# One kernel, one edit: the third block's weight quads in another order, with twelve weight sums read where they were made

## The chip, the cores and the metric

The kernel runs on one core of one Trainium2 chip. The time is the device time of one execution in microseconds; the measured figure is the median over several executions. A core has a matrix engine (TensorE, PE in the profile, with its weight loads as PEld), VectorE (DVE), ScalarE (ACT), GpSimd (POOL) and SyncE (SP). Each has its own instruction stream; they meet in semaphores. Weights and activations lie in on-chip memory (SBUF); TensorE writes into eight accumulation banks (PSUM, numbered 0 to 7), which another engine must read out before they are opened again. Transfers between DRAM and SBUF are issued by SP, ACT or POOL.

## What is computed

The input `x` is 2048 rows of 1024 values. Everything is in bfloat16 outside, and the output is bfloat16.

```python
xn = layernorm(x)                                   # over the 1024 values, no gain or offset
# branch A: a diagonal state space model with 1024 complex states
dt = exp(log_dt);  Lam = Lambda_re + 1j * Lambda_im
Lam_bar = exp(dt * Lam)
B_bar = ((Lam_bar - 1) / Lam)[:, None] * (B_re + 1j * B_im)
Bu = xn @ B_bar.T
h_t = Lam_bar * h_(t-1) + Bu_t                      # over the 2048 rows
y = 2 * real(hseq @ (C_re + 1j * C_im).T) + xn * Dskip
# branch B: a layer of width 3584
z = mish(xn @ w1 + b1) @ w2                         # mish(h) = h * tanh(softplus(h))
out = x + y + z
```

## The kernel before

**Five queues.** The program doesn't issue instructions as it goes. It records each operation in one of five lists (class `Queue`, L91), with the buffers that it reads and writes; from these it derives the semaphore waits, and at the end `emit` (L130) writes each list out as one engine's instruction stream. So the order of the calls in the source is the order on every engine, and an instruction that waits holds up everything that is behind it on its own engine.

**Blocks.** The rows are worked in four blocks of 512. For each block: layernorm; the product with `w1` and, between its parts, the product with the input matrix B; Mish; the scan over the rows; the products with `w2` and with C into the same banks; the output. The first block is plain. The second takes 12 of its 28 tiles of `w1` plainly and the other 16 as four quads (below). The third and the fourth block take all 28 as seven quads. The change is in the third block, whose product with `w1` and B, "the projection", runs in the profile from 306.6 to 373.5 us, and whose output products end at 446.8 us.

**Quads and units.** A quad is four tiles of `w1`, 512 columns. Columns and the inner dimension are halved, and the four quarter products are made with seven multiplications in place of eight (Strassen's scheme in Winograd's form). Each multiplication is a unit, numbered 1 to 7: eight matmuls of 128x256. Units 1, 2 and 4 use weights as they are; units 5, 6, 7 and 3 use sums and differences of weights, made by VectorE (`w_sums`, L1191, the instruction at L1199), always in the order 5, 7, 6, 3. Each is written over one of the raw quarters on chip and then stored to DRAM (array `wsd`) by POOL, except that the stores of group 2 are kept back and issued by SP. The stored units are loaded again for later blocks. The matching sums of the activations are in `TT`. The product with B is cut the same way into four parts of seven units.

**The letters.** The order within a projection is written by hand in strings, one for each block (`STEPS`, L196, for the third). A letter and a number is a step. `p q s w x y z` with 1 to 7 are units of the seven quads, `a b c d` with 1 to 7 those of the product with B. `k0` makes the next sum that is due (first the twelve of the `w1` groups 2, 0 and 1, four each, in this order; then sums for `w2`). `m1` loads raw rows of `w2` by POOL, `h` scales such a row on ScalarE (L1240), which POOL then stores (L1230). `g` is the Mish over a quad's results (L894), preceded by its table load. `r` is a step that prepares the scan on VectorE (L910), `E` the layernorm statistics of one quarter of the next block's rows (L564), `G` a scaling of activations, `t` sums of activations, `S` a scaling of rows, and `l0` the loads of the next block's `x`, four DMAs on POOL (L398). `O0` issues a store that was kept back, on SP: block outputs and the sums of group 2. `D` and `kp` belong to the part after the projection.

`project_fast` (L1368) reads such a string. For each unit `w_product` (L998) records the matmuls (L1024) and `w_evacuate` (L1030) at once what reads the bank out: a snapshot to SBUF on ScalarE (L1044) or on VectorE (L1047, always two instructions), or a join with an earlier snapshot on VectorE (L1061). For B these are `product` (L948 the matmuls), and `evacuate` with copies on VectorE (L963) and ScalarE (L965) and joins (L973).

**Banks.** Each quad has three banks. Unit 1 opens the first, and 6, 7 and 4 add to it; unit 2 opens the second, unit 5 the third, and 3 adds to that. Which three is in `W_BANKS` (L206), in the order of the quads:

```python
W_BANKS = ((0, 2, 1), (3, 2, 4), (7, 2, 6), (3, 5, 7), (1, 5, 6), (4, 5, 7), (3, 5, 6))
```

A unit that opens a bank waits until its last user's result has been read out; one that adds to it waits until the snapshot of the sum so far is out.

**The ring.** Weights come through a ring of seven slots of 512 KB, in the order of use, by SP (`ring_load` L426, `ring_fill` L856). One slot holds two units, each a load of 256 KB. When the last unit of a slot has been used, the slot's place goes to the next item of the list. One group of the second block reads its sums where VectorE made them (`ON_CHIP`); in the third block every unit is loaded through the ring, also those of groups 0, 1 and 2, whose sums are made early in this very projection and go to DRAM and back.

**Which quad is which group.** `REAL` (L207) is (3, 4, 5, 6, 0, 1, 2): in the third and fourth block `p` is group 3, and the groups 0, 1 and 2 are the last three quads, `x`, `y` and `z`.

**Behind the projection** the third block runs `tail` (L1495): matmuls for the fast part of `w2` (L1563) and for its plain part and C (L1502); results kept aside by VectorE in `KS` (L1580) or by ScalarE; scans on VectorE (L1453); and at the end the sums into the output (L1707).

Of the kernel before, what the change touches and what calls it, by code (L numbers as in the profile page):

```python
# [5 lines left out]
ALU = mybir.AluOpType  # L6
# [3 lines left out]
P = 128  # L10
# [153 lines left out]
def build_kernel(nc, A_x, A_Lambda_re, A_Lambda_im, A_B_re, A_B_im, A_C_re, A_C_im,  # L164
# [22 lines left out]
    W2_ORDER = (*range(9), 13, *range(9, 13))  # L187
    EARLY, LATE = ((0, 18), (26, 28)), ((18, 26),)
# [3 lines left out]
    WHOLE = ("a2 a1 V0 b2 b1 a5 b5 V1 P4 P5 a6 b6 v6 P6 P7 a3 b3 P0 a7 b7 P1 Q0 n0 p1 q1 a4 b4 "  # L192
# [6 lines left out]
    LAST = ("p1 p5 p2 q1 q5 p6 q2 s1 p7 s5 p3 q6 s2 M5 p4 q7 q3 k0 k0 s6 q4 g0 K0 a2 a1 k0 s7 k0 s3 O0 O0 O0 O0 m6 b2 b1 s4 G1 G0 g1 a5 G3 b5 G2 a6 b6 "  # L199
# [11 lines left out]
    OPENS = [(REAL[QUADS.index(o[0])], int(o[1])) for o in WHOLE.split() if o[0] in QUADS]  # L211
    OPENS = [u for u in OPENS if u not in ON_CHIP]
    O_ITEMS = [("w1", f // 2) for f in TILES[::2]] + [("ws", tuple(OPENS[i:i + 2])) for i in range(0, len(OPENS), 2)]
# [198 lines left out]
    items = []  # L412
    for blk in range(NB):
        items += W_ITEMS if blk in SPLIT else O_ITEMS if blk == FAST else [("w1", g) for g in range(NF // 2)]
# [8 lines left out]
        items += [("c", j) for j in range(NJ)] if blk >= FAST else []  # L423
    n_loaded = [0]
# [175 lines left out]
    def plain_root():  # L600
        aop(lambda e: e.activation(ln[:, 3, :], mv[:, :, 1], AF.Sqrt, bias=kon[:, 2:3]), reads=b_mv + [b_kon], writes=b_ln[3])
        vop(lambda e: e.reciprocal(ln[:, 3, :], ln[:, 3, :]), reads=b_ln[3], writes=b_ln[3])
        vop(lambda e: e.scalar_tensor_tensor(out=ln[:, 4, :], in0=mv[:, :, 0], scalar=-1.0, in1=ln[:, 3, :], op0=ALU.mult, op1=ALU.mult),
            reads=b_mv + b_ln[3], writes=b_ln[4])
# [245 lines left out]
    n_item = [0]  # L850

    def item_done():
        n_item[0] += 1
        ring_fill()
# [8 lines left out]

    def first_tile(blk, f):
        bank = f % 8
        raw = blk == 0 and f < NR
        if raw:
            first_rest(f)
        for k in range(0 if raw else NK):
            s, w = w1_tile(n_item[0], f % 4, k)  # L870
            PE.mm(lambda e, k=k, w=w: e.matmul(ps[:, bank, :], lhsT=w, rhs=xnT[:, k, :],  # L871
                                               start=k == 0, stop=k == NK - 1),
                  reads=[b_ring[s]] + b_xnT, writes=[b_ps[bank]], first=k == 0, last=k == NK - 1)
        if f % 4 == 3:
            item_done()
            item_done()
        at = place(blk, f)
        ts = slice(2 * P if raw else 0, 4 * P)
        aop(lambda e: e.activation(at[0][:, ts], ps[:, bank, ts], AF.Mish, bias=b1(f)),
            reads=[b_ps[bank], b_par], writes=[at[1]])  # L880
# [113 lines left out]
    def w_out(blk, i, ci):  # L994
        f0 = 4 * i + 2 * ci
        return f0, *(places(SPLIT[0], f0, 2) if blk in SPLIT else places(blk, 4 * REAL[i] + 2 * ci, 2))

    def w_product(blk, i, n):  # L998
# [3 lines left out]
        direct = blk == FAST and (REAL[i], n) in ON_CHIP  # L1002
        if direct:
            unit, b_unit = w_unit(w_raw(REAL[i], *((1, 1), (0, 0), (0, 1), (1, 0))[(5, 6, 3, 7).index(n)]))
        else:
            kind, units = items[n_item[0]]
# [20 lines left out]
        if not direct and half == len(units) - 1:  # L1027
            item_done()
# [219 lines left out]
    def d2_scale(g):  # L1248
        for n in range(4):
            d2_row(4 * g + n)  # L1250
# [789 lines left out]
```

## Time and profile before

| | |
|---|---|
| times of three executions | 588.1, 587.55, 587.74 us |
| median | 587.74 us |
| profiled execution, span | 586.3 us |
| TensorE busy | 581.0 us, 99% of the span |
| VectorE busy | 513.4 us, 88% |
| ScalarE busy | 401.8 us, 69% |
| GpSimd busy | 150.7 us, 26% |
| moved by DMA | 162.15 MB, mean 277 GB/s |

The profile is of one execution. Its span, 586.3 us, is from the first to the last instruction; no device time is given for that execution itself, and the three times are of others. Times in the rows count from the start of the span. A row of the timeline gives the start, the duration, the engine, the line of the code, the operation, what it writes and reads, the shape and how many instructions are drawn together (x8); in brackets stands how long the engine was idle before it, and for whom it waited. A row of a stretch of time gives the stretch, its length, and then for TensorE, its weight loads, VectorE, ScalarE and GpSimd the busy time and the number of instructions, and at its end the granted clock of TensorE, the share of time that the DMA engines were busy, and GB/s. A row of waits gives who waited for whom, the sum in us, the count and the mean. A row of DMAs gives the transfer, who issued it, the count, the size and the median time from issue to landing.

Consecutive matmuls overlap, and their ends are modelled; their starts are what the hardware recorded.

### The profile page before, as it was taken

To read this page: it belongs to the slowest core of one execution; us is meant where nothing else is said; L and a number is where in the kernel's file an instruction comes from. 1 tells how busy PE (TensorE), PEld (TensorE's weight loads), DVE (VectorE), ACT (ScalarE), POOL (GpSimd) and SP (SyncE) were. 2 spreads that over 40 slices of the span, in tenths; PEclk is the share of its full clock that TensorE was granted. 3 is DMA by queue.
4 is the path that set the end of the run, shared out by engine and by line. 5 is a ranking of instruction groups with operands and counts; after the bars stand their busy time and mean duration, and the time that the engine had idled before them with its cause. 6 is when DMAs were issued, how large, how long until landed. Compare 5 with 4: busy or idle time off the path is not lost.

```text
span 586.3 us, 9768 instructions
## 1 busy us (share of the span) xinstructions
PE 581.0 (99%) x3599; PEld 353.9 (60%) x3635; DVE 513.4 (88%) x789; ACT 401.8 (69%) x541; POOL 150.7 (26%) x213
## 2 busy tenths in 40 slices
PE   9999999999999999999999999999999999999998
PEld 8644444444447887444448888644446888844444
DVE  6998999998997878999877889779999669789995
ACT  4859994658578868999916687959223798992330
POOL 2899300123524420441351241001010113100000
PEclk9999999999999999999999999999999999999999
DMA  9999998999688978999999899798865966998832
GB/s 244 306 243 247 245 186 202 316 301 360 185 303 287 357 249 293 316 321 255 345 375 345 305 309 382 257 344 209 306 210 191 346 237 241 326 324 318 293 113 73
DMA packets 116345, 162.15 MB, mean 277 GB/s; under 512 B 55882, under 2 KB 66762, under 8 KB 116298
## 3 DMA queue, kind: packets, MB, share of 16 engines
q1 hardware_dynamic: 99776, 109.67, 62.0%
q0 software_dynamic: 13440, 44.57, 21.7%
q10 hardware_dynamic: 3082, 7.29, 3.3%
q8 instruction: 29, 0.48, 0.3%
q14 instruction: 18, 0.15, 0.1%
HBM read 115.36 MB, written 34.08 MB: 255 GB/s over the span
## 4 chain that ended last, share of the span: by engine, by line
PE 93%; DVE 2%; ACT 2%; DMA 1%; issue 1%; POOL 0%; ACTq 0%; POOLq 0%
PE ps L1502 34%; PE ps L1024 19%; PE ps L948 13%; PE ps L1563 10%; PE ps L871 10%; PE ps L1438 5%; DMA act<-in_A_B_im_dram 1%; PE ps L680 1%; PE ps L689 1%; PE ps L642 1%; ACT act L894 1%; PE ps L1525 1%; ACT act L901 1%; DVE CT L835 0%; DVE CT L833 0%
## 5 line engine op out<-in xcount | busy, mean ns | idle before, releaser
L1502 PE MATMUL ps<-ring,act 128*128 128x512 bf16 x532 | 117.3, 379 | 0.6
L1502 PEld LDWEIGHTS ps<-ring,act 128*128 128x128 bf16 x544 | 53.2, 98 | 63.8
L1044 ACT ACTIVATE snaps<-ps,par,cs 128x256 f32<-128x256 f32 x100 | 54.4, 562 | 44.4 <-PE ps L1024 40.0
L1502 PE MATMUL ps<-ring,hT 128*128 128x512 bf16 x355 | 78.3, 379 | 0.4
L1024 PE MATMUL ps<-TT,ring 128*128 128x256 f16 x552 | 68.3, 273 | 0.0
L910 DVE TENSOR_TENSOR mt<-hT,tab 128x2048 bf16<-128x2048 bf16 (+1 forms) x56 | 67.9, 1213 | 0.4
L1502 PEld LDWEIGHTS ps<-ring,hT 128*128 128x128 bf16 x362 | 35.4, 98 | 42.7
L1453 DVE TENSOR_TENSOR_SCAN hT<-cs,qi,hT 128x512 bf16<-128x512 f32 x48 | 60.7, 1275 | 0.0
L1024 PEld LDWEIGHTS ps<-TT,ring 128*128 128x128 f16 (+1 forms) x552 | 53.8, 98 | 7.2 <-issue 0.2
L871 PE MATMUL ps<-xnT,ring 128*128 128x512 bf16 x258 | 56.8, 379 | 0.3
L1024 PE MATMUL ps<-xnT,ring 128*128 128x256 bf16 x424 | 53.9, 273 | 0.0
L1061 DVE SCALAR_TENSOR_TENSOR act<-ps,cs,snaps 128x512 bf16<-128x512 f32 x54 | 39.8, 748 | 15.2 <-PE ps L1024 13.3
L1024 PEld LDWEIGHTS ps<-xnT,ring 128*128 128x128 bf16 (+1 forms) x424 | 41.4, 98 | 5.4
L871 PEld LDWEIGHTS ps<-xnT,ring 128*128 128x128 bf16 x264 | 25.8, 98 | 30.9
L1230 POOL DMA_DIRECT2D w2d<-act x21 | 15.0, 718 | 110.5 <-ACT act L1240 54.9
L1473 ACT ACTIVATE hT<-hT,wz 128x1024 bf16<-128x1024 bf16 x16 | 18.1, 1146 | 34.3 <-DVE hT L1468 34.3
L1563 PE MATMUL ps<-ring,act 128*128 128x512 bf16 (+1 forms) x176 | 39.5, 379 | 0.2
L1230 POOL DMA_DIRECT2D w2d<-hb x28 | 20.0, 717 | 74.4 <-ACT hb L1240 33.0
L894 ACT ACTIVATE act<-act 128x2048 bf16<-128x2048 bf16 (+3 forms) x13 | 33.0, 2557 | 3.8 <-DVE act L1047 3.8
L973 DVE TENSOR_TENSOR hT<-ps,snaps 128x512 f16<-128x512 f32 x36 | 23.8, 687 | 12.3 <-ACT snaps L965 11.1
L1563 PEld LDWEIGHTS ps<-ring,act 128*128 128x128 bf16 (+1 forms) x180 | 17.6, 98 | 20.6
L1173 POOL DMA_DIRECT2D wsd<-hb x35 | 19.1, 548 | 39.0 <-DVE hb L1199 28.8
(240 smaller groups left out, 1085.2 us busy)
## 6 DMA issues: line engine op xcount, KB each, us to landing
ring<-wsd SPq DMA_DIRECT2D x122, 256.0 KB, 4.6
ring<-in_B_w_dram SPq DMA_DIRECT2D x54, 512.0 KB, 5.9
ring<-ctd SPq DMA_DIRECT2D x24, 512.0 KB, 4.4
ring<-w2d SPq DMA_DIRECT2D x24, 512.0 KB, 4.6
wsd<-hb POOLq DMA_DIRECT2D x35, 256.0 KB, 5.1
ring<-w2d SPq DMA_DIRECT2D x29, 256.0 KB, 3.8
w2d<-hb POOLq DMA_DIRECT2D x28, 256.0 KB, 5.5
w2d<-act POOLq DMA_DIRECT2D x21, 256.0 KB, 6.2
```

Of the source, the lines that this page charges most:

```text
L871: PE.mm(lambda e, k=k, w=w: e.matmul(ps[:, bank, :], lhsT=w, rhs=xnT[:, k, :], start=k == 0, stop=k == NK - 1), reads=[b_ring[s]] + b_xnT, ...
L894: aop(lambda e: e.activation(t, t, AF.Mish), reads=b, writes=b)
L910: vop(lambda e: e.tensor_tensor(mt[:], u.unsqueeze(1).to_broadcast([P, 2, 2, TB]), tab[:, :, j, :].unsqueeze(2).to_broadcast([P, 2, 2, TB] ...
L948: PE.mm(lambda e, w=w, x=x, o=o, begin=begin, end=end: e.matmul(ps[:, bank, o:o + TH], lhsT=w, rhs=x, start=opens and begin, stop=end, ski ...
L1024: PE.mm(lambda e, w=w, x=x, o=o, begin=begin, end=end: e.matmul(ps[:, bank, o:o + TH], lhsT=w, rhs=x, start=opens and begin, stop=end, ski ...
L1044: aop(lambda e, o=o, p=p, j=j: e.activation(o, p, AF.Identity, scale=ig, bias=b1(f0 + j)), reads=[b_ps[b], b_par, b_ig], writes=b_dst)
L1061: vop(lambda e: e.scalar_tensor_tensor(out=dst, in0=bank(b), scalar=ig, in1=src, op0=ALU.mult, op1=ALU.add), reads=[b_ps[b], b_snap[k], b_ ...
L1230: PO.dma(lambda e: e.dma_start(w2d[at // 4][:, at % 4 * TB:(at % 4 + 2) * TB].rearrange("p (j t) -> p j t", j=2), t[:, :, d, :]), sem, rea ...
L1438: PE.mm(lambda e, j=j, ci=ci, k=k, bank=bank: e.matmul(ps[:, bank + ci, :], lhsT=BT[:, ci, j, k, :], rhs=xnT[:, k, :], start=k == 0, stop= ...
L1453: vop(lambda e: e.tensor_tensor_scan(out=hT[:, ci, j, :], data0=cj("r", j).to_broadcast([P, TB]), data1=hT[:, ci, j, :], initial=init, op0 ...
L1502: PE.mm(lambda e: e.matmul(ps[:, u, :], lhsT=lhsT, rhs=rhs, start=st_, stop=last, skip_group_check=blk in SPLIT), reads=reads, writes=[b_p ...
L1563: PE.mm(lambda e: e.matmul(ps[:, bank, :], lhsT=lhsT, rhs=rhs, start=st_, stop=end, skip_group_check=True), reads=b_t + [b_ring[s]], write ...
```

## The change

Four things change, all in the third block or in how its order is written.

1. `REAL` becomes (3, 2, 0, 1, 4, 5, 6). In the third and fourth block the quads `q`, `s` and `w` are now groups 2, 0 and 1, and `x`, `y` and `z` are 4, 5 and 6. The second block keeps its groups (`group`).
2. In the third block units 5, 6, 3 and 7 of groups 2, 0 and 1 are read from the buffers where VectorE made them, not through the ring (`ON_CHIP`). So 12 items of 256 KB are no longer in this block's list. The stores to DRAM stay, for the fourth block.
3. The fourth quad, `w`, stands before and among the first units of the product with B. Before, it came behind all four parts but the last units of `c` and `d`.
4. The order is written out further. What reads a bank out is a step of its own (`ep1` for `p1`), and no longer follows the unit at once; and what lies behind the projection, until the block's output, stands in the same strings. One loop, `perform`, runs all four blocks. A slot of the ring is given on when its last use has been recorded, counted for each item (`used`, `release`). Stores of sums that were kept back and stores of outputs that were kept back are two lists (`O` and `o`).

For the second half of the third block the new string moves, among others: the preparing step `r4` in between the two `KS` steps `kp0` and `kp1`, some scans ahead of others, and the statistics `E3` behind the first half of unit 7 of `w2` (`D70`). The number of matmuls is the same in every block, and the strings for the other three blocks give the order that they had.

The core of the diff:

```diff
-    W2_ORDER = (*range(9), 13, *range(9, 13))
-    EARLY, LATE = ((0, 18), (26, 28)), ((18, 26),)
+    W2_ORDER = tuple(range(14))
+    EARLY, LATE = ((0, 20),), ((20, 28),)
...
-    STEPS = ("p1 p5 p2 k0 k0 q1 k0 q5 p6 k0 q2 s1 k0 p7 s5 p3 k0 q6 s2 p4 k0 q7 q3 k0 s6 q4 m1 k0 g0 a2 a1 k0 s7 O0 s3 O0 b2 b1 k0 O0 s4 g1 k0 O0 a5 "
-             "b5 O0 a6 b6 O0 a3 h4 b3 S0 O0 a7 O0 h5 b7 k0 c2 d2 k0 h6 a4 b4 h7 l0 k0 c5 c1 k0 d5 d1 r0 c6 G0 c3 G1 d6 d3 c7 G2 w1 d7 r1 w5 w2 G3 c4 d4 k0 E0 E1 w6 x1 x5 x2 k0 w7 k0 w3 r2 "
-             "x6 w4 k0 y1 y5 y2 x7 x3 E2 E3 y6 x4 z1 z5 g2 z2 y7 y3 z6 G7 y4 g6 z3 z7 u0 t0 G8 u2 G9 z4 I2 G10 u1 t1 t2")
+    STEPS = ("p1 p5 ep1 ep5 p2 ep2 k0 k0 q1 eq1 p3 k0 q5 p6 q2 k0 ep6 eq2 s1 eq5 O0 k0 ep3 p7 es1 O0 ep7 s5 es5 k0 O0 q6 eq6 s2 es2 O0 p4 ep4 k0 q7 eq7 s6 "
+             "q3 eq3 k0 es6 q4 eq4 g0 k0 s7 s3 es7 o0 w1 ew1 es3 o0 s4 es4 k0 w2 m1 o0 o0 k0 w5 k0 ew2 b1 ew5 b2 eb2 eb1 w6 ew6 w3 b5 eb5 ew3 w7 ew7 ea2 "
+             "a2 g1 a1 ea1 b6 eb6 w4 ew4 a5 b3 h4 ea5 eb3 a6 h5 b7 ea6 eb7 S0 ec2 a3 a7 ea7 k0 ea3 k0 h6 c2 d2 a4 ea4 ed2 b4 h7 c5 eb4 ec5 c1 ec1 k0 d5 "
+             "ed5 d1 ed1 k0 r0 c6 ec6 G0 G1 c3 ec3 d6 ed6 d3 ed3 c7 G2 ec7 l0 x1 ex1 r1 d7 G3 ed7 x5 ex5 c4 x2 E1 ex2 ec4 k0 d4 E0 ed4 x6 y1 ex6 ey1 y5 "
+             "ey5 k0 y2 ey2 x7 ex7 x3 ex3 y6 r2 x4 ey6 ex4 k0 E2 z1 ez1 z5 ez5 z2 y7 y3 ez2 ey7 ey3 z6 z3 ez6 g2 k0 y4 ey4 G7 g6 ez3 z7 G9 ez7 D10 D11 G8 "
+             "z4 t0 ez4 G10 D70 E3 t1 t2 kp2 r3 D20 D71 kp0 g7 r4 G4 lr0 G12 D21 li0 X5 kp1 G5 r5 r6 r7 G11 ns0 X6 kp3 pl24 ns2 pl10 ns1 G6 tr0 ns3 tr1 "
+             "tr2 pl8 tr3 ph8 sc20 sc00 pl22 sc21 ph22 G13 pl12 pl26 sc50 sc01 sc10 to0 sc11 so0 al0 ta0 X3 to1 so1 sc30 al1 to2 sc41 sc31 so2 to3 sc60 "
+             "sc40 al2 so3 sc71 to4 X4 so4 sc51 to5 so5 al4 k0 sc70 al3 sc61 al5 to6 so6 jk0 to7 so7 sk0 al7 sk1 sk2 sk3 al6 Y0 sx0 sx1 sx2 sx3 k0 Y1 Y2 "
+             "Y3 Y4 Y5 k0 Q0 fin0 Q1 fin1 ax2 ax3 Q2 fin2 Q3 fin3")
...
-    REAL = (3, 4, 5, 6, 0, 1, 2)
-    UNITS = [(REAL[QUADS.index(o[0])], int(o[1])) for o in STEPS.split() if o[0] in QUADS]
-    W_ITEMS = [("ws", tuple(UNITS[i:i + 2])) for i in range(0, len(UNITS), 2)]
-    ON_CHIP = [(5, n) for n in (5, 6, 3, 7)]
...
+    REAL = (3, 2, 0, 1, 4, 5, 6)
+
+    def group(blk, i):
+        return REAL[i] if blk in SPLIT else i + 3
+
+    def fetched(blk, order, made):
+        us = [(group(blk, QUADS.index(o[0])), int(o[1])) for o in order.split() if o[0] in QUADS and len(o) == 2 and o[1].isdigit()]
+        us = [u for u in us if u not in made]
+        return [("ws", tuple(us[i:i + 2])) for i in range(0, len(us), 2)]
+
+    ON_CHIP = {FAST: [(5, n) for n in (5, 6, 3, 7)], SPLIT[0]: [(g, n) for g in (2, 0, 1) for n in (5, 6, 3, 7)], NB - 1: []}
...
-    def item_done():
-        n_item[0] += 1
-        ring_fill()
...
+    def used(i):
+        left[i] -= 1
+        if left[i] == 0:
+            gone.add(i)
+            return True
+        return False
+
+    def release():
+        while n_item[0] in gone:
+            n_item[0] += 1
+            ring_fill()
...
     def w_product(blk, i, n):
...
-        direct = blk == FAST and (REAL[i], n) in ON_CHIP
+        g = group(blk, i)
+        direct = (g, n) in ON_CHIP[blk]
         if direct:
-            unit, b_unit = w_unit(w_raw(REAL[i], *((1, 1), (0, 0), (0, 1), (1, 0))[(5, 6, 3, 7).index(n)]))
+            unit, b_unit = w_unit(w_raw(g, *((1, 1), (0, 0), (0, 1), (1, 0))[(5, 6, 3, 7).index(n)]))
...
-        if not direct and half == len(units) - 1:
-            item_done()
+        if not direct and used(at):
+            release()
```

More of the change, by code (lines that the diff above doesn't have):

```diff
@@ L411, in build_kernel @@
     NT = 7 * (NF // 2)
[L412 removed]
+    items, item_blk = [], []
     for blk in range(NB):
[L414 removed]
+        items += W_ITEMS[blk] if blk in SPLIT else O_ITEMS if blk == FAST else [("w1", g) for g in range(NF // 2)]
         if blk == NB - 1:
@@ L850, in build_kernel @@
     n_item = [0]
-    def item_done():
-        n_item[0] += 1
-        ring_fill()
+    at_item, left, gone = {}, {}, set()
+    for i_, (kind_, g_) in enumerate(items):
+        b_ = item_blk[i_]
+        if kind_ == "ws":
+            for u_ in g_:
+                at_item[b_, "ws", u_] = i_
+            left[i_] = len(g_)
+        elif kind_ == "tp":
+            for h_, u_ in enumerate(g_):
+                at_item[b_, "tp", u_] = i_, h_
+            left[i_] = 4 * len(g_)
+        else:
+            at_item[b_, kind_, g_] = i_
+            left[i_] = 2 * min(4, NT - 4 * g_) if kind_ == "ts" else 16
+    def used(i):
[8 more added lines that the diff above has]
+            ring_fill()
     def ring_fill():
@@ L862, in ring_fill @@
             ring_load()
[L864 to L874, printed above, removed]
-            item_done()
[L876 to L880, printed above, removed]
     def places(blk, f, n):
@@ new lines, in perform @@
+        for o in (FIRST, WHOLE, STEPS, LAST)[blk].split():
+            kind = o.rstrip("0123456789.")
+            arg = o[len(kind):]
+            if kind in ("D", "X"):
+                a = arg.split(".")
+                ks = range(int(a[1]), int(a[2])) if len(a) > 1 else range(ng)
+                n, i = (int(a[0][0]), (int(a[0][1]),)) if kind == "D" else (int(a[0]), (0, 1))
+                rows(n, i, ks)
+            elif len(kind) == 1 and kind in QUADS:
+                w_product(blk, QUADS.index(kind), int(arg))
+            elif len(kind) == 1 and kind in "abcd":
+                product(blk, "abcd".index(kind), int(arg))
+            elif len(kind) == 2 and kind[0] == "e" and kind[1] in QUADS:
+                w_evacuate(blk, QUADS.index(kind[1:]), int(arg), keep)
+            elif len(kind) == 2 and kind[0] == "e" and kind[1] in "abcd":
+                evacuate("abcd".index(kind[1:]), int(arg), keep, kind[1:] in "ab" and blk != FAST)
+            else:
+                run[kind](int(arg or 0))
@@ L2005, in build_kernel @@
+        assert near or not (steps or later), (len(steps), len(later))
+    for blk in range(NB):
+        perform(blk)
     SP.wait(out_events.values())
```

763 lines of the change are left out of this document (265 added, 498 removed), and 30 rows, old and new, of tables (FIRST, LAST, WHOLE).

## The prediction

> **What bounds the kernel now.** I read the page's busy times first, then the same by stretches, then who waited for whom on TensorE.
>
> ```profile
> span 586.3 us, 9768 instructions
> PE 581.0 (99%) x3599; PEld 353.9 (60%) x3635; DVE 513.4 (88%) x789; ACT 401.8 (69%) x541; POOL 150.7 (26%) x213
> 306.60:373.50 66.90, 66.89 (x610) 59.43 (x609) 57.16 (x97) 49.33 (x72) 15.93 (x25) 1.00 0.97 335
> PE ps L642 <- DVE filler L468: 1.0, 1, 1.0
> PE ps L680 <- ACT xr L527: 0.2, 1, 0.2
> ```
>
> The third row is the projection of the third block (us from 306.6 to 373.5): TensorE 66.89 of 66.90 us, clock 1.00, DMA share 0.97. The last two rows are all that TensorE is shown to wait for, both at the start. So the sum of the matmuls sets the time, and another engine counts only where it is too late for TensorE. Small waits hide in the modelled ends, so I take them from starts, in the timeline of TensorE:
>
> ```profile
> 306.68 1.04 PE L1024 MATMUL ps<-xnT,ring 128*128 128x256 bf16 x8
> 307.56 1.04 PE L1024 MATMUL ps<-TT,ring 128*128 128x256 f16 x8
> 308.43 1.91 PE L1024 MATMUL ps<-xnT,ring 128*128 128x256 bf16 x16
> 311.92 1.91 PE L1024 MATMUL ps<-xnT,ring 128*128 128x256 bf16 x16
> 313.79 1.91 PE L1024 MATMUL ps<-TT,ring 128*128 128x256 f16 x16
> 332.27 1.92 PE L948 MATMUL ps<-xnT,SS 128*128 128x256 bf16 x16
> 372.45 1.04 PE L1024 MATMUL ps<-TT,ring 128*128 128x256 f16 x8
> ```
>
> A unit (eight matmuls) takes 0.873 us: six of them lie between 306.68 and 311.92. Unit k of the third block should start at 306.68 + 0.8735 (k-1). The 76th, z7, starts at 372.45 instead of 372.19: all waits of this projection are worth 0.26 us. About half is before p7 (due 313.67, started 313.79), half before a3 (332.27).
>
> **The change, part by part.**
>
> *Work.* Each block keeps its seven-product units, tiles, w2 products and output products; only order and source change. TensorE's sum of matmuls is unchanged. The most that can be won in the third block is the 0.26 us.
>
> *Twelve loads less.* Units 5, 6, 3 and 7 of groups 2, 0 and 1 come from where VectorE left them; 12 loads of 256 KB (3.1 MB) go from SP's queue. TensorE waits for no load, so this is worth nothing in itself. The stores stay, because the last block fetches these units.
>
> *New waits on VectorE.* TensorE now waits for the sums themselves. I laid VectorE's new order out with durations and starts of these rows:
>
> ```profile
> 308.02 1.12 DVE L1047 TENSOR_SCALAR snaps<-ps,cs,par 128x256 f32<-128x256 f32 x2
> 309.50 0.75 DVE L1061 SCALAR_TENSOR_TENSOR act<-ps,cs,snaps 128x512 bf16<-128x512 f32 x1 [0.36 <-PE ps L1024]
> 310.17 2.86 DVE L1199 TENSOR_TENSOR act<-act 128x1024 f16<-128x1024 bf16 x4
> 313.00 0.75 DVE L1061 SCALAR_TENSOR_TENSOR act<-ps,cs,snaps 128x512 bf16<-128x512 f32 x1
> 313.66 0.68 DVE L1199 TENSOR_TENSOR hb<-hb 128x1024 f16<-128x1024 bf16 x1
> 331.53 2.48 DVE L963 COPY snaps<-ps 128x512 f32<-128x512 f32 x4
> 310.38 3.27 ACT L1044 ACTIVATE snaps<-ps,par,cs 128x256 f32<-128x256 f32 x6 [0.58 <-PE ps L1024]
> 324.14 1.28 ACT L894 ACT_TABLE_LOAD   x1
> 325.44 3.19 ACT L894 ACTIVATE act<-act 128x3584 bf16<-128x3584 bf16 x1
> ```
>
> A join (L1061) can begin 1.07 us after its unit's start (p2: 308.43, join 309.50) and lets the next instruction begin 0.66 later; a sum (L1199) takes 0.68. From VectorE's end to TensorE's start it is 0.06 us (a copy of 0.68 from 331.53, then 332.27); from ScalarE 0.14 (six snaps end at 313.65, p7 at 313.79). Then:
>
> - q5 is unit 6, due 311.05. The group's first sum runs 310.17 to 310.85 as before: 0.14 to spare.
> - s5 is unit 11, due 315.42. q2 (unit 8) starts at 312.80, its join 313.87, the sum 314.54 to 315.22: 0.14 to spare.
> - s6, unit 16, due 319.79: join of s2 318.24, sum 318.90 to 319.58: 0.15. s3, unit 20, due 323.28: join of q3 321.73, sum to 323.07: 0.15.
>
> Each deadline hangs on a join that itself follows TensorE, so a delay isn't carried on. Cost: nothing, cover 0.14 us.
>
> *The fourth quad earlier.* W_BANKS gives s the banks (7, 2, 6) and w (3, 5, 7). s4 fills bank 7, and w5, which opens bank 7, is now two units behind it; before, 24. s4's result goes out on VectorE in two L1047 instructions. s4 is unit 22, start 325.03; VectorE is free, so it begins 326.10, needs 1.12 and 0.06: w5 can start at 327.28. It is due 326.77. **Cost 0.51 us.** Behind it everything is 0.51 later, which also covers ScalarE: the snap of w1 now stands behind the first Mish. q4's evacuation ends 323.76; the table (1.28) and Mish (3.19) end 328.33; w1's snap ends 329.5, for w6, now due 329.90: 0.24 to spare. w5's snap ends 330.6, for w3, due 330.78: 0.04 to spare with the 0.14. These are the thinnest covers. I take zero for them; the other end is 0.3 if each handover is 0.1 slower.
>
> *Waits removed.* p7 is unit 10 instead of 9 and p6's snap is out at 314.15, for 314.54: the first 0.12 goes. a5's copy is out 1.7 us before a3: the second 0.14 goes. Together -0.26.
>
> *Queues.* SP gets the four stores of group 2 and block 1's outputs in another place; ring loads behind them are for units 30 us ahead, so zero. On POOL the raw w2 rows (m1) wait for the stores of group 0's sums, issued by 323.7. The store row below says 6.0 us, so they leave near 329.6 against 328.60 before; ScalarE scales them from 338.2, as two 512 KB loads took 6.1 us: zero, cover 2 us.
>
> ```profile
> ring<-wsd SPq DMA_DIRECT2D x122, 256.0 KB, 4.6
> wsd<-hb POOLq DMA_DIRECT2D x8, 256.0 KB, 6.0
> hb<-in_B_w_dram POOLq DMA_DIRECT2D x2, 512.0 KB, 6.1
> 328.60 1.44 POOL L1225 DMA_DIRECT2D hb<-in_B_w_dram  x2 [5.32 <-DMA wsd<-hb]
> 339.76 2.21 POOL L1230 DMA_DIRECT2D w2d<-hb  x3
> 341.96 2.20 POOL L398 DMA_DIRECT2D xx<-in_A_x_dram  x4
> 352.87 1.41 DVE L564 BATCH_NORM_STATS2 stats<-xx 128x6 f32<-128x512 bf16 x2
> DMA to landing us min/median/max: 2.9/7.4/11.3
> ```
>
> The next block's x is asked for later: "l0" moves from behind b4 to behind c7. On POOL it stands behind the store of the sixteenth sum, which VectorE ends at 351.2; x of q1 leaves at 352.5. VectorE wants it at 357.6 ("E1" behind r1 and the join of d7). The last row is for all loads of x in the kernel: 2.9 to 11.3 us. In the third block now it took the upper end, with five stores issued in the 3.7 us before it and ring loads beside it. In the new order TensorE sits on units long loaded from w4 to x5, so SP loads nothing between 337 and 356; I take 4.7 us, nearer the minimum: 357.2, no wait. Later units follow the same arithmetic with 0.2 us or more to spare.
>
> *The second half* (w2, output). VectorE sets how late the block's end is:
>
> ```profile
> 388.00 1.41 DVE L1580 SCALAR_TENSOR_TENSOR KS<-ps,wz,xx 128x512 f32<-128x512 f32 x2 [2.77 <-PE ps L1563]
> 397.70 3.63 DVE L1453 TENSOR_TENSOR_SCAN hT<-cs,qi,hT 128x512 bf16<-128x512 f32 x3
> 443.46 2.47 DVE L1707 SCALAR_TENSOR_TENSOR xx<-ps,wz,KS 128x1024 bf16<-128x1024 f32 x2
> 450.82 0.74 DVE L1061 SCALAR_TENSOR_TENSOR act<-ps,cs,snaps 128x512 bf16<-128x512 f32 x1
> ```
>
> Now it idles 2.77 us ahead of 388.00 and has no rest from there to 450.82. The new order takes r4 into that gap, so the scans begin near 396.1 instead of 397.70, even with E3 moved in behind D70. TensorE is not late there now; 1.6 us more of cover changes nothing in the time.
>
> *Sum.* 0.51 - 0.26 = +0.25 us on a span of 586.3: 586.55. The page gives no time for this execution beside its span; the median of the runs, 587.74, lies 1.44 above, and I carry that: **588.0 us**, range of this case 587.7 to 588.6. About 0.2% (1.2 us) is what a measurement of this kernel can tell from no change.
>
> **Rivals.**
>
> *x comes late (slower).* If q1's x lands after t = 358.35, E1 holds VectorE, and the joins of x2 and x7 behind it come after y2 and x4 want their banks (E1 1.57, five more instructions of 0.6 to 0.75, E0 1.57; x4 due 364.8). Price t - 358.35: with the median of 7.4, t = 359.9 and 1.6 us, 589.6; with 10.4, 592.5. Against it: the empty queue. For it: the two medians of 6 us leave hardly any slack. It leaves the 0.2% from t = 359.3.
>
> [...]
>
> *The handovers are slower than read.* q5, s5, s6, s3, q7, w6 and w3 each lose 0.1 to 0.2: 588.3 to 589.2.
>
> *No wait before w5.* If bank 7 comes free in time, only the 0.26 is won: 587.5, within the bound. That the twelve loads do nothing is in the forecast already.
>
> **How the numbers follow.** Forecast 0.52, all within 0.2%. No wait 0.06, within. Slower handovers 0.12, half of it within. x late 0.20, of which 0.03 within. POOL blocked 0.06, slower. Something that I don't see and that makes it faster by over 0.2%: 0.04, since no wait of that size is there to remove. So same 0.52 + 0.06 + 0.06 + 0.03 = 0.67, slower 0.06 + 0.17 + 0.06 = 0.29, faster 0.04. The range 587.4 to 590.0 holds the forecast, the case without a wait, the handovers and x up to t = 360.1; outside remain about 0.15.
>
> **What would show it.** A gap of half a us on TensorE at w5 (about 326.8 to 327.3), with VectorE's pair of L1047 before it; no gap before p7 and a3; sums ending 0.1 to 0.2 us before q5, s5, s6 and s3; 110 loads in the row of ring<-wsd instead of 122; E1 starting directly behind the join before it; z7 starting near 372.7; scans 1.5 us earlier. I'm wrong if VectorE waits for a DMA ahead of E1, if several gaps stand in the first 28 units, or if TensorE waits behind 373.

## The result

| | before | changed |
|---|---|---|
| median | 587.84 us | 590.13 us |
| executions | 587.55 to 588.1 (5) | 588.62, 588.97, 590.13, 591.52, 591.8 |
| profiled execution | span 586.3 us | 588.62 us, span 587.4 us |

The ratio is 1.004, with a 95% interval of 1.0025 to 1.0055: the change makes the kernel slower by 0.4%. The forecast was 588.0 us in a range of 587.4 to 590.0. Two things are to be explained: the profiled execution, the shortest of the five, has a span 1.1 us longer than before instead of 0.25; and the executions lie 3.2 us apart, where before they lie within 0.6. (Ratios here and below leave out executions that count as slow, which is one alone: the 596.7 us of other_both.)

The profile after: the span, the two stretches of the third block, TensorE's waits in them, and a row of DMA issues.

```profile
span 587.4 us, 9770 instructions
306.60:373.50 66.90, 66.55 (x610) 59.30 (x608) 55.05 (x92) 49.00 (x71) 15.49 (x25) 1.00 0.78 271
373.50:446.80 73.30, 72.82 (x343) 33.18 (x341) 69.99 (x92) 37.02 (x44) 4.69 (x7) 1.00 0.80 258
PE ps L1064 <- DVE act L1087: 0.3, 1, 0.3
PE ps L1544 <- issue: 0.2, 1, 0.2
PE ps L1544 <- DMA ring<-w2d: 0.2, 1, 0.2
ring<-wsd SPq DMA_DIRECT2D x110, 256.0 KB, 4.2
```

The DMA share of the projection fell from 0.97 to 0.78, and 110 loads are left of 122. TensorE now waits in both stretches. Line numbers moved: L1064 is the unit's matmul (L1024 before), L1087 VectorE's snapshot (L1047), L1239 the sum of weights (L1199), L1297 the sum of w2 (L1261), L1270 its store (L1230), L1265 the load of raw w2 rows (L1225), L1280 their scaling (L1240), L1544 the matmul of w2 (L1563 and L1502), L1676 the output addition (L1711). The starts show how much it waits:

```profile
325.91 1.04 PE L1064 MATMUL ps<-xnT,ring 128*128 128x256 bf16 x8
327.29 1.05 PE L1064 MATMUL ps<-TT,hb 128*128 128x256 f16 x8 [0.35 <-DVE act L1087]
326.12 1.12 DVE L1087 TENSOR_SCALAR act<-ps,cs,par 128x256 bf16<-128x256 f32 x2 [1.00 <-PE ps L1064]
377.92 1.89 PE L1544 MATMUL ps<-ring,S 128*128 128x512 f16 x8
380.05 1.02 PE L1544 MATMUL ps<-ring,act 128*128 128x512 bf16 x4 [0.24 <-issue]
381.31 1.04 PE L1544 MATMUL ps<-ring,act 128*128 128x512 bf16 x4 [0.23 <-DMA ring<-w2d]
382.19 1.03 PE L1544 MATMUL ps<-ring,S 128*128 128x512 f16 x4
```

The first two rows: w2 starts at 325.91, so w5 was due at 326.78 and starts at 327.29. That is 0.51 us, behind the pair of snapshots in the third row. Four matmuls of w2 take about 0.87 us (381.31 to 382.19). So the two rows behind 377.92 were due at 379.66 and 380.92 and started 0.39 us late each, about 0.8 together. Before, the same products follow each other without a gap:

```profile
377.65 1.89 PE L1563 MATMUL ps<-ring,S 128*128 128x512 f16 x8
379.38 1.89 PE L1563 MATMUL ps<-ring,act 128*128 128x512 bf16 x8
381.11 1.89 PE L1563 MATMUL ps<-ring,S 128*128 128x512 f16 x8
```

There is no gap before p7 or a3 (they were worth 0.26 us before). 0.51 + 0.8 - 0.26 = 1.05 us, which accounts for the 1.1 us of span.

SyncE's queue tells what the 0.8 us is. Below are its wait between 330 and 385 us, and the stores that GpSimd issues for the w2 sums of the second row group (the first three of four), after and then before:

```profile
SPq L482 <- DMA w2d<-hb: 4.1, 1, 4.1
360.76 0.72 POOL L1270 DMA_DIRECT2D w2d<-hb  x1 [6.17 <-DVE hb L1297]
363.08 0.73 POOL L1270 DMA_DIRECT2D w2d<-hb  x1 [1.60 <-DVE hb L1297]
367.78 0.71 POOL L1270 DMA_DIRECT2D w2d<-hb  x1 [3.97 <-DVE hb L1297]
```

```profile
353.27 0.71 POOL L1230 DMA_DIRECT2D w2d<-hb  x1 [7.68 <-DVE hb L1261]
357.89 0.72 POOL L1230 DMA_DIRECT2D w2d<-hb  x1 [3.92 <-DVE hb L1261]
358.99 0.71 POOL L1230 DMA_DIRECT2D w2d<-hb  x1 [0.37 <-DVE hb L1261]
```

The sums are steps `k0` of the string. Spread further back, the third of them is stored 8.8 us later. The three stores share one semaphore (`d_ts`, three DMAs each), so SyncE's load for product 7, which needs the second sum only, waits until the third has landed. SyncE gets to it at 368.6 and stands for 4.1 us, with all the loads of w2 behind it. That this wait is the 0.8 us is so far an inference; sem_split tests it.

None of this explains the scatter. That took the experiments.

### The profile page after: what moved, and what is told of

Its sections match the earlier page's. It is cut to its first block, busy times and chain, and to the rows that moved or that the text cites. A ratio compares the mean times of both kernels' runs of the same rounds, so it can differ in the third digit from the quotient of the medians.

```text
span 587.4 us, 9770 instructions
## 1 busy us (share of the span) xinstructions
PE 582.3 (99%) x3635; PEld 352.9 (60%) x3635; DVE 512.4 (87%) x784; ACT 401.8 (68%) x541; POOL 150.4 (26%) x213
## 4 chain that ended last, share of the span: by engine, by line
PE 97%; DMA 2%; DVE 0%; SPq 0%; issue 0%
PE ps L1544 49%; PE ps L1064 18%; PE ps L986 12%; PE ps L1755 10%; PE ps L1773 5%; PE ps L714 1%; PE ps L723 1%; DMA ring<-w2d 1%; DMA ring<-in_B_w_dram 1%; DVE act L1087 0%; PE ps L548 0%; SPq L433 0%; PE ps L583 0%; DVE xx L1709 0%; SPq L429 0%
## 5 line engine op out<-in xcount | busy, mean ns | idle before, releaser
L1544 PE MATMUL ps<-ring,act 128*128 128x512 bf16 (+1 forms) x724 | 158.1, 379 | 0.5 <-issue 0.2
L1544 PEld LDWEIGHTS ps<-ring,act 128*128 128x128 bf16 (+1 forms) x724 | 70.7, 98 | 85.3 <-DMA ring<-w2d 0.7
L1544 PE MATMUL ps<-ring,hT 128*128 128x512 bf16 (+1 forms) x390 | 83.4, 376 | 0.0
L1544 PEld LDWEIGHTS ps<-ring,hT 128*128 128x128 bf16 x390 | 38.1, 98 | 45.0
L1064 PE MATMUL ps<-TT,ring 128*128 128x256 f16 x480 | 59.8, 273 | 0.0
L1101 DVE SCALAR_TENSOR_TENSOR act<-ps,cs,snaps 128x512 bf16<-128x512 f32 x54 | 39.5, 747 | 16.7 <-PE ps L1064 14.9
L1064 PEld LDWEIGHTS ps<-TT,ring 128*128 128x128 f16 (+1 forms) x480 | 46.9, 98 | 6.2
L1064 PE MATMUL ps<-xnT,ring 128*128 128x256 bf16 x400 | 50.6, 273 | 0.0
L1270 POOL DMA_DIRECT2D w2d<-act x21 | 15.0, 715 | 110.9 <-DVE act L1297 47.1
L1064 PEld LDWEIGHTS ps<-xnT,ring 128*128 128x128 bf16 (+1 forms) x400 | 39.0, 98 | 5.1
L1270 POOL DMA_DIRECT2D w2d<-hb x28 | 20.0, 716 | 76.6 <-ACT hb L1280 33.2
L1011 DVE TENSOR_TENSOR hT<-ps,snaps 128x512 f16<-128x512 f32 x36 | 24.0, 687 | 13.6 <-ACT snaps L1003 12.2
L1766 ACT ACTIVATE act<-ps,par 128x512 bf16<-128x512 f32 (+1 forms) x40 | 23.7, 662 | 8.2 <-PE ps L1755 8.1
L939 ACT ACTIVATE act<-act,cs 128x512 bf16<-128x512 bf16 x44 | 28.1, 709 | 0.1
```

Source lines behind the costliest of these rows:

```text
L939: aop(lambda e, a=a, y=y: e.activation(a, a, AF.Copy, scale=y), reads=[b_a, b_y], writes=[b_a])
L1064: PE.mm(lambda e, w=w, x=x, o=o, begin=begin, end=end: e.matmul(ps[:, bank, o:o + TH], lhsT=w, rhs=x, start=opens and begin, stop=end, ski ...
L1101: vop(lambda e: e.scalar_tensor_tensor(out=dst, in0=bank(b), scalar=ig, in1=src, op0=ALU.mult, op1=ALU.add), reads=[b_ps[b], b_snap[k], b_ ...
L1270: PO.dma(lambda e: e.dma_start(w2d[at // 4][:, at % 4 * TB:(at % 4 + 2) * TB].rearrange("p (j t) -> p j t", j=2), t[:, :, d, :]), sem, rea ...
L1544: PE.mm(lambda e: e.matmul(ps[:, bank, lo:hi], lhsT=lhsT, rhs=rhs, start=opens, stop=last, skip_group_check=split), reads=reads, writes=[b ...
```

## The experiments

Medians in us; "before" is the kernel before on the same chip in the same job. "Long" counts executions above 591. The ratio is not that of the two medians: the long executions weigh in it too.

| run | n | median | lowest to highest | long | before | ratio, 95% interval |
|---|---|---|---|---|---|---|
| again | 7 | 593.66 | 588.55 to 595.4 | 5 | 587.81 | 1.008 [1.0051, 1.0109] |
| sem_split | 12 | 588.71 | 587.57 to 595.39 | 3 | 587.81 | 1.0036 [1.0009, 1.0062] |
| sums_early | 8 | 591.78 | 589.9 to 596.54 | 4 | 587.81 | 1.0086 [1.0057, 1.0114] |
| x_early | 10 | 589.15 | 588.58 to 596.12 | 4 | 587.81 | 1.0056 [1.0028, 1.0083] |
| other_rows | 12 | 591.07 | 587.66 to 596.23 | 6 | 588.06 | 1.0049 [1.0024, 1.0074] |
| other_raw | 11 | 589.55 | 588.99 to 596.38 | 5 | 588.06 | 1.0054 [1.0029, 1.0079] |
| other_both | 11 | 591.1 | 587.66 to 596.7 | 6 | 588.06 | 1.0039 [1.0016, 1.0062] |
| before_late | 11 | 588.11 | 587.75 to 588.83 | 0 | 588.06 | 1.0001 [0.9992, 1.0009] |
| old_rows | 7 | 589.01 | 588.28 to 590.26 | 0 | 587.86 | 1.0025 [1.0015, 1.0036] |
| load_later | 11 | 589.2 | 588.6 to 590.09 | 0 | 587.86 | 1.0023 [1.0014, 1.0031] |
| before_rows | 12 | 589.36 | 587.82 to 596.13 | 4 | 587.86 | 1.0049 [1.0021, 1.0077] |
| all_three | 11 | 587.69 | 587.18 to 588.34 | 0 | 587.86 | 0.9997 [0.9988, 1.0005] |

### First round: is it the wait of SyncE, or x?

**again** is the changed kernel, unaltered.

> The changed kernel once more. Its five times lay between 588.62 and 591.8, those of before within 0.4 us. My theory: SyncE stands in front of a load of w2 until the store of a w2 sum has landed (4.1 us in the profiled run), and this landing varies. So a profile of a slower execution shows a longer wait on SyncE's queue for w2d<-hb and longer gaps on TensorE between 379 and 383 us, about 0.8 us plus what the time is above 588.6, and nothing else new. Rival (x late): a slower execution shows VectorE waiting for xx<-in_A_x_dram ahead of E1, and gaps on TensorE between 360 and 366 us.

The scatter is real and larger than first seen: up to 595.4. But the profiled execution was again the shortest (588.55), with 3.8 us on SyncE's queue (4.1 in the first profile) and 0.3 us of waits on TensorE at w2 (0.4 there, worth 0.8 by the starts). So the profile said nothing on the long ones; three of them carry a mean granted clock of 0.997 instead of 1.0.

**sem_split** gives the third store a semaphore of its own.

```diff
-        sem = DmaSem(nc, "d_ts%d" % g, nper=3)
+        sem = DmaSem(nc, "d_ts%d" % g, nper=2)
         last = DmaSem(nc, "d_tu%d" % g)
+        own = DmaSem(nc, "d_tv%d" % g)
...
-                d2_store(g, n, h, d, last if n == 4 else sem)
+                d2_store(g, n, h, d, {4: last, 6: own}.get(n, sem))
```

> As the changed kernel, but the store of each group's third w2 sum (for product 6) has a semaphore of its own; the load for product 7 then waits for the stores of the first two sums alone, the second of which is issued about 5 us earlier. VectorE's order is untouched. My theory: SyncE's wait of 4.1 us falls below 0.6, the gaps of 0.41 and 0.40 us on TensorE at 379.4 and 380.7 go, the gap of 0.51 at 326.7 stays; 588.0 to 588.2 us, with all times within 0.6 us. Rival (x late, or VectorE's new order as such): nothing changes, 589 to 592.

In the profile both gaps near 380 are gone, and so is SyncE's wait for w2d<-hb; span 586.3 us, time 587.57.

```profile
377.70 1.89 PE L1545 MATMUL ps<-ring,S 128*128 128x512 f16 x8
379.42 1.89 PE L1545 MATMUL ps<-ring,act 128*128 128x512 bf16 x8
381.15 1.89 PE L1545 MATMUL ps<-ring,S 128*128 128x512 f16 x8
```

So the 0.8 us is this semaphore. But three of twelve executions were still at 592.4 to 595.4: half of my theory fell.

**x_early** issues the loads of x where they were before.

```diff
-... ed2 b4 h7 c5 ... c7 G2 ec7 l0 x1 ...
+... ed2 b4 h7 l0 c5 ... c7 G2 ec7 x1 ...
```

> As the changed kernel, but the loads of the next block's x are issued where they were before (behind b4). My theory: VectorE had no wait for x in the profiled run, so this gains nothing: 588.6 to 592 as before, the wait on SyncE's queue stays at 3 to 6 us. Rival x late: 588.0 to 588.2 us with a scatter below 0.6.

Four of ten at 593 or more: x is not the cause either.

**sums_early** makes the w2 sums sooner by moving the statistics E1 and E0 back.

```diff
-... x2 E1 ex2 ec4 k0 d4 E0 ed4 x6 ... ey5 k0 y2 ... ex4 k0 E2 ...
+... x2 ex2 ec4 k0 d4 k0 ed4 x6 ... ey5 k0 y2 ... ex4 E1 E0 E2 ...
```

> As the changed kernel, but the statistics E1 and E0 give up their places to the next w2 sums and come where the third of these sums stood: the third sum then ends near 362 instead of 367.4 us. My theory: the store lands near 367.5, before SyncE needs it (368.6), so 588.0 to 588.2 us and no gap at 379 to 381. Rival x late: also better, since E1 comes 6 us later; so this run alone does not part them, sem_split and x_early do. If only the landing of stores is slower in the new order, the time stays above 589.

```profile
PE ps L1064 <- DVE act L1101: 1.2, 1, 1.2
PE ps L1064 <- DVE snaps L1087: 0.6, 1, 0.6
```

SyncE's wait for the store is gone as expected, but the two rows of TensorE's waits show what I overlooked: E1 and E0 in one piece, ahead of E2, hold VectorE for some 3 us (each took 1.57 us in the changed kernel's profile) in front of the joins and snapshots of the last quads. The shortest execution became 589.9, where 588.0 was expected. The long ones stayed.

### Second round: which load, if any?

Two more places where SyncE waits for stores were left: late w2 sums altogether (A), or raw units 1, 2 and 4 of groups 2, 0 and 1, which are stored at the end of the second block and now wanted much sooner (B). These kernels read data that landed long ago instead, and so compute something else.

```diff
             for h, u in enumerate(g):
+                if u % 7 == 1 and u // 7 in (1, 3, 4, 6):
+                    u -= 1
...
             for h, (i, n) in enumerate(g):
+                if item_blk[n_loaded[0] - 1] == SPLIT[0] and i < 3 and n in (1, 2, 4):
+                    i = 3
```

**other_rows** has the first edit, **other_raw** the second, **other_both** both.

> As the changed kernel, but in the third block the loads of the sums of w2's second row group (products 7, 5, 6 and 4) read the first row group's sums instead, which landed long before; the output is another one. Every sum is still made and stored, so VectorE, GpSimd and the transfers are the same; only the wait of SyncE for the landing of late sums is gone. Theory A (the scatter is this wait): 588.0 us, all executions within 0.7 us, like before. Theory B (the scatter is another wait, for the raw units 1, 2 and 4 of groups 2, 0 and 1, which are stored at the end of the second block and are now fetched 20 to 40 us earlier): lowest at 587.6 to 588.1, but a third or more of the executions still at 592 to 596.

> As the changed kernel, but in the third block the loads of the raw units 1, 2 and 4 of groups 2, 0 and 1 read group 3's, which landed in the first blocks; the output is another one. Theory A: nothing changes, 588.6 at the least and executions up to 595. Theory B: the long executions go, all lie at 588.5 to 589.5 (the wait for the w2 sums costs its 0.8 us still).

> Both: no load in the third block waits for a store of this block or of the end of the second. Theories A and B: 588.0 us, all executions within 0.7 us. If long executions stay, neither set of loads is the cause, and something else in the new order is (the loads of x, raw rows of w2, or a place where no engine waits in the profiled execution).

All three scatter as before, so neither A nor B. By its own expectation, other_both says that it is something else, and here the profiled execution was a long one at last (594.99, span 593.8, mean clock 0.994). It is the only long execution that was profiled. Its lines are four further down than in the changed kernel. TensorE, VectorE and ScalarE in it, at the end of the second block (the raw rows of w2 are scaled on ScalarE, summed on VectorE, and only then the output is added and the banks come free):

```profile
304.76 2.11 PE L1548 MATMUL ps<-ring,hT 128*128 128x512 bf16 x9
312.01 1.86 PE L1068 MATMUL ps<-xnT,ring 128*128 128x256 bf16 x8 [5.15 <-DVE xx L1680]
313.67 1.91 PE L1068 MATMUL ps<-TT,ring 128*128 128x256 f16 x8
295.41 4.27 ACT L1284 ACTIVATE act<-act,cs 128x1024 bf16<-128x1024 bf16 x4 [8.49 <-DMA act<-in_B_w_dram]
307.79 2.94 DVE L1301 TENSOR_TENSOR act<-act 128x1024 f16<-128x1024 bf16 x4 [10.81 <-DMA w2d<-act]
310.65 4.61 DVE L1680 TENSOR_TENSOR xx<-ps,xx 128x1024 bf16<-128x1024 f32 x4
```

Read from below: VectorE's output additions begin at 310.65, since the sums ahead of them waited 10.81 us; those are written over the scaled rows and waited for their stores, the stores waited for ScalarE, and ScalarE had waited 8.49 us for GpSimd's load of raw w2 rows. So the third block's first unit starts at 312.01 instead of 306.70, which is 5.3 us. The first eight matmuls then take 1.66 us (312.01 to 313.67) instead of 0.87. A table by stretches shows why (TensorE, weight loads, VectorE, ScalarE, GpSimd; at the end granted clock, DMA share, GB/s):

```profile
306.60:312.00 5.40, 0.26 (x2) 0.02 (x1) 4.04 (x6) 0.00 (x0) 3.17 (x5) 0.72 1.03 393
312.00:316.00 4.00, 3.99 (x20) 2.80 (x21) 3.96 (x5) 0.38 (x1) 0.00 (x0) 0.52 1.04 409
316.00:320.00 4.00, 4.00 (x39) 3.57 (x38) 3.50 (x6) 1.88 (x4) 0.00 (x0) 1.00 0.92 349
```

The granted clock is 0.52 for 4 us after the wait, which costs 0.48 x 4 = 1.9 us. 5.3 + 1.9 = 7.2 us of the 7.4 between this span and that of the kernel's shortest execution (593.8 and 586.4). The clock fell during the wait: it is 1.00 from 296.00 to 306.60, 0.72 in the mean from 306.60 to 312.00, 0.52 in the next 4 us, and 1.00 again from 316.00. If it was 1.00 up to the fall and 0.52 from there on, it fell some 2.2 us into the first of these stretches, near 308.9 (an estimate from these rows).

The raw rows come in four loads of 512 KB. Below are, for this kernel and then for the kernel before: GpSimd's issue of the first of them; the time to landing of SyncE's four DMA transposes of `xn`, which fill `xnT` for the next block (issued from 262 to 276 us); and the stretch from 280 to 290 us.

```profile
272.63 0.72 POOL L1269 DMA_DIRECT2D act<-in_B_w_dram  x1 [1.93 <-PE ps L1548]
...
DMA to landing us min/median/max: 4.1/8.9/16.7
...
280.00:290.00 10.00, 10.00 (x48) 4.54 (x47) 9.38 (x24) 6.92 (x4) 1.80 (x3) 1.00 1.10 166
```

```profile
276.06 0.72 POOL L1225 DMA_DIRECT2D act<-in_B_w_dram  x1 [5.38 <-PE ps L1502]
...
DMA to landing us min/median/max: 4.3/4.8/5.7
...
280.00:290.00 10.00, 9.95 (x47) 4.53 (x47) 9.38 (x24) 10.00 (x8) 2.34 (x4) 1.00 1.01 383
```

The first load leaves 3.4 us earlier. It overwrites the activation tiles 20 to 23, and waits until w2 has read them. That they are read earlier is the first line of the diff: with `W2_ORDER` natural, row tiles 26 and 27 come last in the second block instead of tenth of the fourteen pairs (the expectations below say ninth), and all between move up by one step of 3.45 us. So the load now leaves together with the transpose issued at 272.6. The DMA engines are as busy as before (1.10 and 1.01) and move less than half (166 and 383 GB/s).

**before_late** is the kernel before with the w2 sums as late as that.

```diff
-... c4 d4 k0 E0 E1 w6 x1 x5 x2 k0 w7 k0 w3 r2 x6 w4 k0 y1 y5 y2 x7 x3 ... y7 y3 z6 ...
+... c4 d4 E0 E1 w6 x1 x5 x2 w7 k0 w3 r2 x6 w4 k0 y1 y5 y2 x7 k0 x3 ... y7 y3 k0 z6 ...
```

> The kernel before with one thing of the change alone: the sums of w2's second row group are made as late as in the changed kernel (about 4, 8 and 10 us later), by moving these four steps back in the string. Theory A: SyncE waits 3 to 5 us for the store of the third sum, TensorE loses 0.3 to 1 us near 380 in the profile, and executions scatter upwards by 2 us or more. Theory B: the wait and the 0.3 to 1 us are there, but the executions stay together within 1 us.

```profile
SPq L450 <- DMA w2d<-hb: 1.7, 1, 1.7
365.07 0.71 POOL L1230 DMA_DIRECT2D w2d<-hb  x1 [2.04 <-DVE hb L1261]
```

The expectation of theory A fails: no gap on TensorE and no scatter. The store leaves at 365.07, not at 367.78, since VectorE has less before it there; SyncE stands for 1.7 us, not for the 3 to 5 expected, and this is still covered. So a wait of 1.7 us costs nothing here and one of 4.1 us costs 0.8: the cover lies between, some 3.3 us by this pair (an estimate). The run does not reach the long wait; what speaks against theory A is other_rows.

### Third round: the order of the w2 rows

Theory C: the long executions come from this collision.

**old_rows** takes back the first two lines of the diff.

```diff
-    W2_ORDER = tuple(range(14))
-    EARLY, LATE = ((0, 20),), ((20, 28),)
+    W2_ORDER = (*range(9), 13, *range(9, 13))
+    EARLY, LATE = ((0, 18), (26, 28)), ((18, 26),)
```

> As the changed kernel, but W2_ORDER, EARLY and LATE as before, so in the second block the w2 rows 26 and 27 come ninth again. Theory C: the natural order frees the four activation tiles that the raw w2 rows overwrite 3.4 us earlier, so GpSimd's load of 512 KB leaves at 272.6 instead of 276.1 us and runs into SyncE's DMA transposes of xn (issued from 272.6); in some executions both then take twice to four times as long, VectorE's sums and output additions at the end of the second block come late, and TensorE waits up to 5 us at 306.5. So with the old order the long executions go: all at 588.4 to 589.6, the 0.8 us at 379 to 381 (wait for the w2 sums) and the 0.51 us at w5 stay. Rival (another cause in the order of the third block): a third or more of the executions at 591 to 596 as now.

No long execution: 588.28 to 590.26, a little wider than expected. The wait for the w2 sums has a spread of its own: in profiles with this wait, TensorE's waits at w2 add up to between 0.3 us (again) and 1.0 (0.6 + 0.4, this run's, at 589.81). The load leaves at 276.60, and the transposes land in 4.4 to 5.6 us.

**load_later** keeps the natural order and makes the load wait for the transposes.

```diff
             queue.dma(lambda e, t=t, src=src: e.dma_start(t.rearrange("p j d t -> p j (d t)"), src), sem, writes=b_t,
+                      reads=b_xnT if g == 2 else ())
```

> As the changed kernel, natural W2_ORDER too, but GpSimd's first load of these raw rows waits until the transposes of xn have landed (one more dependency), so it leaves near 279 us. Theory C: transposes land in 4 to 6 us again, no long executions, 588.4 to 589.6. If only the order of rows itself matters, not the load: still 591 to 596 in a third or more.

```profile
281.14 2.85 POOL L1265 DMA_DIRECT2D act<-in_B_w_dram  x4 [10.16 <-DMA xnT<-xn]
...
DMA to landing us min/median/max: 4.5/4.7/5.2
```

All four loads leave from 281.14 on, later than in the other kernels, and yet ScalarE, VectorE and TensorE are in time: eleven executions at 588.6 to 590.09. So not the order of rows does it, and not too little time for the load, but its company. SyncE's loads of `ctd` are in this stretch here too (six issued between 266 and 300 us, landing after 4.5 us in the median); the transposes have landed.

**before_rows** puts the collision into the kernel before, with nothing else.

```diff
-    W2_ORDER = (*range(9), 13, *range(9, 13))
+    W2_ORDER = (*range(9), 13, 10, 11, 9, 12)
```

> The kernel before with one thing changed: W2_ORDER (0 to 8, 13, 10, 11, 9, 12), so that the tiles that the first raw load overwrites are read one step (3.45 us) earlier, as in the changed kernel; EARLY and LATE stay. Nothing of the third block changes. Theory C: the load leaves at 272.6 us, and a third or more of the executions lie 3 to 8 us above 587.8. Rival: all executions at 587.2 to 589.1 like before.

Its load leaves at 272.86, and four of twelve executions lie at 592.25 to 596.13, with clocks of 0.994 to 0.997; three more lie at 589.3 to 590.5. The others are at 587.8 to 588.2, where the kernel before is. Theory C holds in both directions, though no long execution of this kernel was profiled.

**all_three** undoes the three losses: the old order of rows, the separate semaphore, and w5 behind b2.

```diff
-... k0 w2 m1 o0 o0 k0 w5 k0 ew2 b1 ew5 b2 eb2 eb1 w6 ew6 w3 b5 eb5 ew3 w7 ew7 ea2 a2 g1 a1 ...
+... k0 w2 m1 o0 o0 k0 b1 k0 ew2 b2 eb2 eb1 w5 ew5 b5 eb5 w6 ew6 w3 ew3 a2 ea2 w7 ew7 g1 a1 ...
```

> The changed kernel with the old W2_ORDER, the semaphore of its own for the third w2 sum, and w5 moved behind b2 (w6, w3, w7 one to two units back, a2 ahead of w7), so that bank 7 is free and ScalarE's snapshots of w1, w5 and w6 are out in time. If my sums of the terms hold (0.8 at the w2 products, 0.51 at w5, the long executions): no gap above 0.1 us on TensorE in the third block, 587.5 us, all within 0.8 us, that is 0.2 to 0.4 below before. If ScalarE's Mish still holds up a snapshot: gaps of 0.1 to 0.6 us ahead of w6, w3 or w7 and 587.7 to 588.1.

```profile
306.60:373.50 66.90, 66.89 (x611) 59.71 (x611) 55.52 (x94) 49.42 (x72) 15.74 (x25) 1.00 0.82 284
```

TensorE's starts show no gap in the third block. The median is 587.69 us against 587.86, ratio 0.9997 [0.9988, 1.0005], and the executions lie 1.2 us apart (0.8 was expected): the losses are gone, but the gain of 0.2 us can't be told from nothing. Twelve loads less and an order without a gap are worth no more, since TensorE had lost only 0.26 us there.

## Why the prediction was wrong

**What held.** The sum of +0.25 us for the projection was right to a few hundredths:

- w5's wait was put at 0.51 us behind the pair of snapshots, and is 0.51. The 0.26 us before p7 and a3 went.
- The sums for q5, s5, s6 and s3 were to be out 0.14 to 0.15 us ahead, and none of the four has a gap.
- E1 was to start at 357.6 with x landed, and it starts there without waiting. ScalarE's scaling of the raw rows starts at 338.18 (338.2 was said). The scans start at 396.44, 1.3 us sooner (1.6 were said).

```profile
338.18 4.25 ACT L1280 ACTIVATE hb<-hb,cs 128x1024 bf16<-128x1024 bf16 x4
357.56 1.41 DVE L596 BATCH_NORM_STATS2 stats<-xx 128x6 f32<-128x512 bf16 x2
xx<-in_A_x_dram POOLq DMA_DIRECT2D x4, 256.0 KB, 3.7
396.44 4.80 DVE L1406 TENSOR_TENSOR_SCAN hT<-cs,qi,hT 128x512 bf16<-128x512 f32 x4
```

- x did not come late: it landed in 3.7 us (4.7 was assumed). The forecast gave 0.06 to a blocked POOL, and no run shows one: GpSimd issued the four loads of x in 2.19 us from 352.40, and they landed after 3.7 us in the median, while VectorE was busy for 3.63 us of those 3.7 (352.4 to 356.1).
- That the twelve loads were worth nothing in themselves holds too.

**The first step that failed: "Queues".** It priced block 1's outputs, the stores of group 2, the raw rows and x on the queues, and closed with "Later units follow the same arithmetic". But the change also moved the last `k0` steps, and each of them issues a store on GpSimd that SyncE waits for. The rows of these stores were in the profile before (353.27, 357.89, 358.99). What was missing is that the load for product 7 hangs on the third store, 8.8 us later now: 4.1 us on SyncE and about 0.8 on TensorE. In the sum, 0.8 stands where the prediction had zero. sem_split takes away this wait alone, and the gaps with it. Among the signs of a wrong prediction the text had this one: that TensorE waits behind 373.

**The second step that failed: "Work".** "Each block keeps its seven-product units, tiles, w2 products and output products; only order and source change." The order that changed was taken to be that of the third block, and the section on the change says so too. `W2_ORDER` is the order of w2's rows in the first two blocks, it stands first in the diff, and it got no price. It frees four tiles 3.4 us sooner, a load leaves sooner, and meets the transposes. The second block's string gives the order that it had, but this tuple beside it does not. Seven of the changed kernel's first twelve executions lie above 591 us; with the load moved away (old_rows, load_later) none of eighteen does. The prediction followed the moved raw rows and x to their queues; the same, done for a load that moves because a wait ends sooner, would have caught it.

**The sum now.** 587.84 + 0.25 (projection, as forecast) + 0.8 (w2 sums) = 588.9 for executions without the collision; old_rows has 589.01 and load_later 589.2. With the collision 0 to 7 us come on top, with a median of the first five at 590.13. That this lies only 0.13 us outside the range is luck: the next seven executions of the same kernel have a median of 593.66.

The range was too narrow since it was made from the third block's unknowns alone, and none of the rivals lay in the second.

## What to carry to other kernels

Go through a diff by what each line frees earlier, not only by what it delays: a buffer that is free sooner lets a DMA leave sooner (here 3.4 us), into whatever runs there. When steps that make data move back, follow each to its store, to the semaphore that the store shares with others, and to the in-order queue that waits for it. And look at the spread of the times before the profile: if it has grown, one profiled execution may not show the cause as a wait (here it showed only in the transposes' time to landing), and an edit that moves the suspected transfer by a few us, in both kernels, finds it.

## What the hardware did that I had not expected

In these runs the DMA transposes from SyncE land later when a load of 512 KB from GpSimd's queue leaves with the third of them and ahead of the fourth, and in the long execution the loads around them land late too. In all nine profiles of kernels that free the four tiles 3.4 us sooner (the load leaves at 272.63 us in the changed kernel's and in the long execution, at 272.86 in before_rows), the slowest transpose lands after 7.1 to 16.7 us (7.5 in the changed kernel's, 11.7 in again's, 16.7 in the long execution). In the five others, where the fourth is already on its way or has landed (the load leaves at 276.06 us in the kernel before, at 276.34 in all_three, 276.60 in old_rows and 281.14 in load_later; the fifth is before_late's), the slowest lands after 5.1 to 5.7. In the long execution the four loads took 12.2 to 19.3 us, against 7.1 to 9.8 in the kernel before, and SyncE's other loads were late too: between 266 and 300 us those of `ctd` took 16.5 us and those of `wsd` 13.2, against 5.5 and 4.7 in the changed kernel's profile (medians). The DMA engines moved 166 GB/s there from 280 to 290 us, with a share of 1.10, against 387 GB/s and 1.05.

So the collision is in every one of the nine (7.1 us at the least, against 5.7 at the most in the five), and only its size differs. TensorE loses by it when it is large: VectorE's sums begin 10.4 us later in the long execution than in the changed kernel's profile (307.79 and 297.38), and TensorE starts 5.3 us later, so some 5 us of lateness are covered (an estimate from this pair). Why the transfers hold each other up, and why so unequally, stays open: the runs show that moving the load away ends it (old_rows, load_later) and that moving it there starts it (before_rows).

In the long execution a wait of 5.15 us on TensorE cost nearly 2 us more than itself (0.48 x 4, an estimate), by a granted clock of 0.52 over the next 4 us; with the wait of 0.51 us in the changed kernel the clock is 1.00 (306.60 to 373.50). Not every long execution lost clock: 593.66 (again) and 593.93 (x_early) have a mean of 1.0.
